# Convolving block 3 token-major in a pair with block 4, with the work around it reordered

## The chip, the cores and the metric

The kernel runs on one core of one Trainium2 chip. The metric is the device time of one execution in microseconds. A core has five engines that run side by side and wait for each other through semaphores: TensorE (PE, matrix products into PSUM), VectorE (DVE), ScalarE (ACT), GpSimd (POOL) and SyncE (SP, which here issues nearly all DMAs). "PEld" in a profile is the loading of weights into PE, which overlaps its products.

## The reference

Two steps follow each other. The first is a light causal convolution over time: x has 8 sequences of 4160 tokens with 192 channels, 8 heads of 24 channels each, and each head has 7 taps that a softmax turns into weights. The second is a feed-forward layer with a maximum of three branches.

```python
w = weight - np.max(weight, axis=-1, keepdims=True)
w = np.exp(w)
w = w / (np.sum(w, axis=-1, keepdims=True) + 1e-09)
x_pad = np.concatenate([np.zeros((B, pad, D)), x], axis=1)
idx = np.arange(S)[:, None] + np.arange(K)[None, :]
x_unf = x_pad[:, idx, :].reshape(B, S, K, H, group)
y = np.einsum('hk,bskhg->bshg', w, x_unf).reshape(B * S, D)
h = np.maximum(np.maximum(y @ w1, y @ w2), y @ w3)      # 192 -> 768
out = h @ w_out                                         # 768 -> 192
```

## The kernel before

The 33280 tokens are cut into 65 blocks of 512 (`NBLK`); block `t` is worked on in turn `t` of a loop that starts at 2, since blocks 0 and 1 are started by hand-written calls ahead of it. All work is in one program for five engines. The order on each engine is the order in which the Python code issues it: the kernel switches automatic scheduling off (`manual_schedule`).

**Convolution, two forms.** Blocks 0 to 3 (`NDENSE = 4`) are convolved densely: `cast_dense` casts x to 16 bit, `conv_dense` (L375) multiplies it with a band matrix in 80 products and gives y with channels on partitions, and `cross` copies half of it across partitions. From block 4 on the convolution is token-major: `cast_x` (L194, on POOL) casts the loaded tile `xf` to a tile `x16`, `conv` (L354) does 64 products for a whole `x16` tile (one block, a pair of blocks, or half the heads of four blocks), `evac` (L394) copies the PSUM tiles `G` to `ys`, `turn` (L408) has SP issue two DMA transposes from `ys` to `yp`, and `double` (L417, on POOL) makes the copy of `yp` in which the two halves of the partitions are swapped. Block 4 is alone in its tile, then pairs (5, 6), (7, 8) and so on follow, and blocks from 13 (`QUADS`) on go by fours. Token-major tiles need rows of zeros between the loaded ones; `zero_x` writes them once into each of the buffers `xf`.

**First product of the feed-forward layer** (`l1`, L500). The maximum of three branches is computed from differences of weights (`wd`). For each of 6 chunks (`j`) of 128 hidden units, three products of 64 rows go into a PSUM tile `lp` and three into `lq`; the two "lanes" use the upper and lower half of the PE rows, at the same time. `top` then evacuates: ACT makes `r = relu(lp)` (L487), DVE makes `h = max(r, lq)` (L488). `lp` lies in pool `psp` and `lq` in pool `psq`, each with 2 buffers of one bank.

**Second product** (`st2`, L564). A block takes 60 products of 192 columns, 30 in each lane, into tiles `po` of pool `psw` (4 buffers); `total` adds the lanes (ACT copy L571, DVE addition L572) for tokens 0 to 255 and for 256 to 511. `st2(t, (a, b))` issues what is left up to product a of lane 0 and b of lane 1.

**Interleaving.** In turn t the loop issues `l1(t, j)` for the six chunks and, after each, a share of `st2(t - 1)`: `EVEN = [5, 10, ..., 30]` or, in a turn with a late convolution, `ROOM`. The lists `convs_at`, `casts` and `loads` say in which turn a block is convolved, cast and loaded; `load_on` issues the loads. `meet()` empties both lanes before other PE work is issued. In turn 2 the kernel before calls `conv_dense(3)` after chunk 1 and `conv` of block 4 after chunk 3; in turn 3, after chunk 1, `conv` of the pair (5, 6).

**Start.** ACT exponentiates the taps and DVE normalises them into `line`; 38 small PE products (L280) spread `line` over `band`, which the convolutions use. `keep_warm` runs products on zeros while PE waits.

Of the kernel before, what the change touches and what calls it, by code (L numbers as in the profile page):

```python
# [10 lines left out]
FP32 = mybir.dt.float32  # L11
# [5 lines left out]
KW = 7  # L17
PAD = KW - 1
NHEAD = 8
# [9 lines left out]
def kernel(  # L29
# [53 lines left out]
                            o_lo - (row_lo - S)))  # L83
        return res

    NDENSE = 4
    chunks_of = [conv_chunks(blk) for blk in blocks[:NDENSE]]
    NQ = len(chunks_of[0])
    TOK = 32
# [28 lines left out]
    def get_x(t):  # L118

        if not 0 <= t < NB or t in xin:  # L120
            return
        if t < XBUF:
            xbuf.append(const.tile([P, NR, D], FP32, name=f"xf_{t}"))
        xf = xbuf[t % XBUF if t < NDENSE + XBUF else NDENSE + (t - NDENSE - XBUF) % 3]
        assert all(v[0] is not xf for v in xin.values())
        xin[t] = [xf, 0, ()]

    def zero_x(t, q0=0, q1=NR, eng=None):

        if t >= NDENSE:  # L130
            get_x(t)
        xf = xbuf[t]
        if eng is not None:
            eng.memset(xf[TOK:HALF, q0:q1, :], 0.0)
            return
        zero = idle[TOK:HALF, 0:D]
        nc.scalar.copy(out=xf[TOK:HALF, q0:q1, :],
                       in_=bass.AP(tensor=zero.tensor, offset=zero.offset,
                                   ap=[list(zero.ap[0]), [0, q1 - q0], [1, D]]))

    def load_x(t, eng=nc.sync):
        if not 0 <= t < NB:
            return
        loaded.add(t)
        get_x(t)
        xf = xin[t][0]
        if t < NDENSE:
            todo = [(0, c[3], c[1] * SEQ + c[2], i) for i, c in enumerate(chunks_of[t])]
        else:
            todo = [(HALF * (i // NR) + (0 if s else LAP), KR if s else TOK,  # L150
                     b * SEQ + s - (LAP if s else 0), i % NR) for i, (b, s) in enumerate(rows_of(t))]
        parts = []
        i, n = 0, len(todo)
        row = [c[2] for c in todo]
        while i < n:
            k = i
            while k + 1 < n and todo[k + 1][:2] == todo[i][:2] and row[k + 1] - row[k] == row[i + 1] - row[i]:
                k += 1
            step = row[i + 1] - row[i] if k > i else 0
            p0, rlen, _, q0 = todo[i]  # L160
            q1 = todo[k][3] + 1
            src = bass.AP(tensor=x.tensor, offset=row[i] * D,
                          ap=[[D, rlen], [step * D, q1 - q0], [1, D]])
            eng.dma_start(out=xf[p0:p0 + rlen, q0:q1, :], in_=src)  # L164
            if parts and parts[-1][0] == rlen:
                parts[-1] = (rlen, parts[-1][1], q1)
            else:
                parts.append((rlen, q0, q1))
            i = k + 1
        xin[t] = [xf, todo[0][0], parts]  # L170

    pairs = {NDENSE: (NDENSE, 0, 1)}
    for t in range(NDENSE + 1, NB):
        u = (t - NDENSE - 1) % 2 if t < QUADS else (t - QUADS) % 4
        pairs[t] = (t - u, u, 2 if t < QUADS else 4)

    def place(t):
# [19 lines left out]
    NC, NSLOT, CYC = D // HALF, D // 32, 96  # L197
    NCH = NC * NBLK // P
    xz = {t: [const.tile([P, NQ, D], FP16, name=f"xz_{t}_{v}") for v in range(2)] for t in range(2)}
    xz[2], xz[3] = xz[0], xz[1]  # L200

    def cast_dense(t, copies, slots_=range(CYC // 32)):
        xf, _, parts = xin.pop(t)
        for v, copy in enumerate(copies):
            if copy is None:
                continue
            for s in slots_:
                cut = GRP * (32 * s // GRP + 1)
                a, b = (32 * s, cut) if v == 0 else (cut, 32 * s + 32)
                for (rl, q0, q1) in parts:  # L210
                    copy(  # L211
                        out=xz[t][v][0:rl, q0:q1, :].rearrange("p q (k c) -> p q k c", c=CYC)[:, :, :, a:b],
                        in_=xf[0:rl, q0:q1, :].rearrange("p q (k c) -> p q k c", c=CYC)[:, :, :, a:b])
# [23 lines left out]
    load_wb(slice(PW, DFF))  # L237
    load_wa(slice(2 * PW, DFF))
    nc.sync.dma_start(out=wos[:], in_=moe_w_out.rearrange("(j p) c -> p j c", p=P))
    load_x(2)  # L240
    load_x(3)
    ident = const.tile([P, P], FP32)
    make_identity(nc, ident[:])
    ident16 = const.tile([P, P], FP16)
    nc.gpsimd.tensor_copy(out=ident16[:], in_=ident[:])
    idle = const.tile([P, NBLK], FP16)
    nc.vector.memset(idle[:], 0.0)
    def keep_warm(n, pool=psw, tag="w"):
# [13 lines left out]
    band = const.tile([P, NHEAD, BAND_W], FP16)  # L262
    nc.vector.memset(band[:], 0.0)
    keep_warm(5, psp, "p")
    wexp = const.tile([NHEAD, KW], FP32)
    wsum = const.tile([NHEAD, 1], FP32)
    nc.scalar.activation(out=wexp[:], in_=wk[:], func=AF.Exp, accum_out=wsum[:])
    wrec = const.tile([NHEAD, 1], FP32)
    nc.vector.reciprocal(out=wrec[:], in_=wsum[:])
    zero_x(4)  # L270
    nc.vector.tensor_scalar_mul(out=line[:, 31:31 + KW], in0=wexp[:], scalar1=wrec[:])
    for v in range(2):
        nc.vector.memset(xz[1][v][:], 0.0)
    cast_dense(0, (nc.vector.tensor_copy, nc.vector.tensor_copy))
# [133 lines left out]
                nc.sync.dma_start_transpose(out=yp[:, 0, i, :, :, :].rearrange("p u k n -> p (u k) n"),  # L408
                                            in_=slots[t][:, i, v:v + n, :, :].rearrange("p u r d -> p (u r d)"))

    def double(t):

        if not NDENSE <= t < NB:
            return
        yp = dense[t]
        for i in range(2):
            nc.gpsimd.tensor_copy(out=yp[HALF * i:HALF * (i + 1), 1, :, :, :, :].rearrange("p i u k n -> p (i u k n)"),  # L417
                                  in_=yp[HALF * (1 - i):HALF * (2 - i), 0, :, :, :, :].rearrange("p i u k n -> p (i u k n)"))

    def spot(t, i, c, r):  # L420

# [32 lines left out]
    def op(fn):  # L454
        ops.append((tuple(put), fn))
# [21 lines left out]
    def meet():  # L477

        emit(True)
        assert not ops  # L480
        clock[0] = clock[1] = 0
# [194 lines left out]
    zero_x(6, 4, NR, nc.vector)  # L676
    conv_dense(0, (ACT, DVE))
    zero_x(6, 0, 4)
    for t in range(NDENSE, XBUF):
        load_x(t)  # L680
    copy_w3(DVE, 0, 2)
    make_wd(2, 0, 2)
# [24 lines left out]
    l1_dense([(1, 4, WW), (1, 5, WW)], "HF")  # L707
    tops((1, 4), (1, 5))
    transpose_w3((PQ[0], PQ[0], PQ[1]))
    cast_dense(3, (GP, GP))  # L710
    cross_wd(1, ACT)
    first_hidden(0)
    first_hidden(1)
# [4 lines left out]
    make_m(1)  # L718
    zero_x(0, NQ)
    zero_x(2, NQ, NR, nc.vector)  # L720
    zero_x(3, NQ, NR, nc.vector)
    load_x(7)
    cast_x(5)

    convs_at = {2: 4, 3: 5, 4: 7}
    convs_at.update({t - 3: t for t in range(9, QUADS, 2)})
    convs_at.update({t - 4 + i: t for t in range(QUADS, NB, 4) for i in range(2)})
    casts = {4: 9}  # L730
# [5 lines left out]
    def load_on(t):  # L736
        for v in range(loads[t - 1] + 1, loads[t] + 1):
            if v not in loaded:
                load_x(v)

    EVEN = [5, 10, 15, 20, 25, 30]
    ROOM = [5, 13, 17, 21, 26, 30]
    OWN, AHEAD = 3, 4
    for t in range(2, NB):
        u = convs_at.get(t, NB)
        late = t > 2 and u < NB
        if t in (3, 4):
            double(t + 1)
        if t > 3:
            for v in range(casts.get(t - 1, 8) + 1, casts[t] + 1):  # L750
                cast_x(v)
        l1(t, 0)
        if t == 2:
            first_rest()
        elif t == 3:
            cast_x(8)
            nc.gpsimd.tensor_copy(out=m16[0:HALF, 2, :], in_=m16[HALF:P, 0, :])
            nc.gpsimd.tensor_copy(out=m16[HALF:P, 2, :], in_=m16[HALF:P, 1, :])
        if t > 3 and not late:
            op(lambda t=t: (store(t - 2, 0, 4, (nc.sync,)),  # L760
                            turn(t + 2, (2,)) if place(t + 2)[1:] == (0, 4) else None, load_on(t)))
        else:
            op(lambda t=t: store(t - 2, 0, 4, (nc.sync,)))
        cuts = ROOM if late else EVEN
        st2(t - 1, (cuts[0], cuts[0]))
        for j in range(1, NJ):
            l1(t, j)
            if late and j == 1:
                st2(t - 1, (cuts[0] + OWN + AHEAD, cuts[0] + OWN))
                meet()  # L770
                quad, second = u >= QUADS, u < QUADS or t == u - 3
                conv(u, WPWQ, range(4 * second, 4 * second + 4) if quad else range(NHEAD))
                for i in (0, 2):
                    evac(u, i)
                for i in (1, 3):
                    evac(u, i, nc.vector.tensor_copy)
                if second:
                    turn(u)
                load_on(t)
            if t == 2 and j == 1:  # L780
                meet()
                conv_dense(3, (ACT, DVE))
                zero_x(1, NQ, NR, nc.vector)
                cross(3, GP)
                load_x(8)
                cast_x(6)
            elif t == 2 and j == 3:
                meet()
                conv(u, WW)
                evac(u, 0)  # L790
                evac(u, 1, nc.vector.tensor_copy)
                turn(4)
                load_x(9)
                cast_x(7)
            st2(t - 1, (cuts[j], cuts[j]))
            if j == 1 and t > 4 and t + 2 in pairs and pairs[t + 2][1] % 2 == 0:
                double(t + 2)
            if t == NB - 1 and j == 3:
                op(lambda: store(NB - 2, 0, 2, (nc.sync,)))
        if t == NB - 1:  # L800
            op(lambda: store(NB - 2, 2, 4, (nc.sync,)))
    last(NB - 1)
# [28 lines left out]
```

## Time and profile before

| | |
|---|---|
| device time, median of 3 runs | 454.51 us (454.46 to 455.02) |
| span of the profiled execution (no own time is given beside it) | 452.8 us |
| median less that span | 1.7 us |
| PE busy | 446.9 us, 99% |
| DVE, ACT, POOL busy | 356.7, 320.0 and 203.0 us |
| granted TensorE clock, mean | 0.999 |

The profile is of one execution. A row of the timeline gives start and length in us, engine, line of the code, operation, output and input, partitions and shape, count, and in brackets how long the engine was idle before it and what ended that. Lengths of PE products include a tail in which the next product already runs, so the cost on PE is read from start to start.

### The profile page before, as it was taken

Reading aid. Unit: us, or ns where it says so; the run is one execution under the profiler, and the core shown is the slowest. Engines: PE = TensorE matmul, PEld = TensorE weight load, DVE = VectorE, ACT = ScalarE, POOL = GpSimd, SP = SyncE. Lnnn points to the kernel's source line nnn. Section 1 sums busy time; section 2 is a strip of 40 time slices with the busy share of each in tenths; the row PEclk is TensorE's granted clock in tenths of the full one; section 3 lists DMA queues with packets and bytes.
Section 4 is the critical chain, followed back from the end, with each engine's and each line's share of the span. In section 5 each row is a group of like instructions: output and inputs, shape, how many; then the busy total and the mean of one; then the engine's idle time right before and its main releaser. Section 6 shows DMA issues by size and latency. Waiting matters only on the chain.

```text
span 452.8 us, 18491 instructions
## 1 busy us (share of the span) xinstructions
PE 446.9 (99%) x7702; PEld 411.5 (91%) x7702; DVE 356.7 (79%) x614; ACT 320.0 (71%) x605; POOL 203.0 (45%) x226
## 2 busy tenths in 40 slices
PE   8999999999999999999999999999999999999997
PEld 4569999999999999999999999999999999999996
DVE  7767778878878788887878788887878788787775
ACT  7767767767777676777767677776767777776664
POOL 2774836556454444635353363444346452504000
PEclk9999999999999999999999999999999999999999
DMA  7978977597966958497585958958594876435223
GB/s 205 231 186 152 225 188 196 143 202 184 171 177 141 178 127 225 123 175 183 119 189 143 192 137 161 199 137 182 135 213 115 178 189 119 116 88 104 59 72 106
DMA packets 127987, 72.03 MB, mean 159 GB/s; under 512 B 52064, under 2 KB 127711, under 8 KB 127903
## 3 DMA queue, kind: packets, MB, share of 16 engines
q1 hardware_dynamic: 127743, 70.75, 69.4%
q8 instruction: 60, 0.98, 1.0%
q14 instruction: 24, 0.20, 0.2%
q10 hardware_dynamic: 160, 0.10, 0.1%
HBM read 33.28 MB, written 25.56 MB: 130 GB/s over the span
## 4 chain that ended last, share of the span: by engine, by line
PE 96%; SPq 2%; DMA 1%; issue 0%; POOL 0%; DVE 0%; POOLq 0%
PE po L564 36%; PE lq L500 31%; PE lp L500 22%; PE G L354 3%; DMA ws<-in_moe_w_dram 1%; PE lw L523 1%; SPq L227 1%; SPq L223 1%; PE D L375 1%; PE po L622 0%; PE po L595 0%; PE lp L523 0%; SPq L164 0%; PE pm L334 0%; POOL wd L299 0%
## 5 line engine op out<-in xcount | busy, mean ns | idle before, releaser
L564 PE MATMUL po<-wo,h 64*128 64x192 f16 x3024 | 331.3, 243 | 0.7 <-issue 0.7
L488 DVE TENSOR_TENSOR h<-r,lq 128x512 f16<-128x512 f16 x384 | 263.0, 686 | 85.9 <-ACT r L487 78.2
L487 ACT ACTIVATE r<-lp 128x512 f16<-128x512 f32 x384 | 229.0, 597 | 115.1 <-PE lp L500 101.8
L500 PE MATMUL lp<-yp,wd 64*128 64x512 f16 x1098 | 295.7, 376 | 0.0
L500 PE MATMUL lq<-yp,wd 64*128 64x512 f16 x1098 | 295.5, 376 | 0.0
L564 PEld LDWEIGHTS <-h 64*128 64x128 f16 x3024 | 241.6, 94 | 6.8 <-issue 4.9
L500 PEld LDWEIGHTS <-wd 64*128 64x128 f16 x2268 | 179.1, 94 | 12.3 <-issue 0.2
L194 POOL CAST x<-xf 103x768 f16<-103x768 f32 x122 | 97.5, 827 | 107.5 <-DMA xf<-in_x_dram 82.0
L564 PE MATMUL po<-m,yp 64*128 64x192 f16 x720 | 141.1, 243 | 0.0
L417 POOL COPY yp<-yp 64x1536 f16<-64x1536 f16 (+1 forms) x62 | 89.6, 1445 | 95.9 <-DMA yp<-ys 70.6
L572 DVE TENSOR_TENSOR o<-a,po 128x384 f32<-128x384 f32 x126 | 69.0, 547 | 0.0
L564 PEld LDWEIGHTS <-yp 64*128 64x128 f16 x720 | 66.3, 94 | 0.3
L571 ACT COPY a<-po 128x384 f32<-128x384 f32 x126 | 59.5, 473 | 0.0
L394 ACT CAST ys<-G 128x384 f16<-128x384 f32 x61 | 26.3, 482 | 9.6 <-PE G L354 9.6
L394 DVE CAST ys<-G 128x384 f16<-128x384 f32 x61 | 31.0, 550 | 0.0
L354 PE MATMUL G<-x,band 39*32 39x192 f16 (+2 forms) x1152 | 17.3, 234 | 0.0
L354 PEld LDWEIGHTS <-band 39*32 39x32 f16 x1152 | 10.7, 91 | 5.2 <-issue 4.7
L500 PE MATMUL lp<-yd,wd 64*128 64x512 f16 x36 | 9.7, 376 | 0.0
L500 PE MATMUL lq<-yd,wd 64*128 64x512 f16 x36 | 9.7, 376 | 0.0
L211 POOL CAST xz<-xf 112x160 f16<-112x160 f32 (+2 forms) x15 | 4.4, 339 | 8.8 <-DVE w3s L303 7.6
L523 PEld LDWEIGHTS <-wd 128*128 128x128 f16 (+1 forms) x48 | 3.0, 96 | 5.6 <-issue 2.2
L375 PEld LDWEIGHTS <-xz 112*32 112x32 f16 x320 | 4.7, 107 | 3.3 <-POOL xz L211 1.3
(72 smaller groups left out, 97.6 us busy)
## 6 DMA issues: line engine op xcount, KB each, us to landing
xf<-in_x_dram SPq DMA_DIRECT2D x113, 234.0 KB
out_dram<-o SPq DMA_DIRECT2D x62, 384.0 KB
xf<-in_x_dram SPq DMA_DIRECT2D x7, 204.8 KB
xf<-in_x_dram SPq DMA_DIRECT2D x3, 420.0 KB
ws<-in_moe_w_dram SPq DMA_DIRECT2D x8, 128.0 KB
yp<-ys SPq DMA_TRANSPOSE x62
out_dram<-o SPq DMA_DIRECT2D x5, 192.0 KB
wos<-in_moe_w_out_dram SPq DMA_DIRECT2D x1, 576.0 KB
```

What stands on the lines that cost most here:

```text
L194: nc.gpsimd.tensor_copy(out=x16s[t0][0:K, :, :, u, r, :].rearrange("p h j c -> p j h c"), in_=xf[0:K, 4 * r:4 * r + 4, :].rearrange("p j ( ...
L354: nc.tensor.matmul(G[2 * (k // per) + i][TOK * j:TOK * (j + 1), k % per, :], lhsT=band[row, h, HALF * i + LAP:HALF * i + KR], rhs=x16s[t0] ...
L375: nc.tensor.matmul(ps[32 * g:32 * g + 32, lo:hi], lhsT=xz[t][v][0:rlen, q, 32 * s:32 * s + 32], rhs=band[0:rlen, h, cc:cc + hi - lo], star ...
L394: copy(out=slots[t][:, i % 2, :, :, GRP * h0:GRP * (h0 + per)].rearrange("p u r (h c) -> p h (u r) c", c=GRP), in_=G[i][:].rearrange("p h ...
L417: nc.gpsimd.tensor_copy(out=yp[HALF * i:HALF * (i + 1), 1, :, :, :, :].rearrange("p i u k n -> p (i u k n)"), in_=yp[HALF * (1 - i):HALF * ...
L487: nc.scalar.activation(out=r[:], in_=ps[0][:], func=AF.Relu)
L488: nc.vector.tensor_max(out=hs[t][:, j, :], in0=r[:], in1=ps[1][:])
L500: nc.tensor.matmul(ps[i][:], lhsT=w_of(i, c, j), rhs=y_all(t, i, c), start=(n == 0), stop=(n == NC - 1))
L523: nc.tensor.matmul(open_ps[t, j, i][:], lhsT=a, rhs=b, start=(t, j, i) not in begun, stop=(t, j, i) in begun)
L564: nc.tensor.matmul(ps[b0, i][:, s % 2, :], lhsT=a, rhs=b, start=first, stop=last)
L571: nc.scalar.copy(out=a[:], in_=ps[s - 1, 0][:])
L572: nc.vector.tensor_add(out=outs[t][:, s - 1:s + 1, :], in0=a[:], in1=ps[s - 1, 1][:])
```

## The change

- `NDENSE` becomes 3. Block 3 is loaded in the token-major layout (its zeros written by POOL near the start, `zero_x(3, eng=nc.gpsimd)`), cast by `cast_x`, and shares one tile with block 4: one `conv(3, ...)` in turn 2 after chunk 1 gives both, into four tiles `G`, evacuated by ACT and DVE, two each. The convolution of block 4 alone and the dense one of block 3 with its `cross` are gone.
- At the end of turn 2 new calls follow: the convolution of the pair (5, 6), its transposes, then the doubling copies of pair (3, 4), the first on POOL and the second on DVE, with the whole second stage of block 2 issued in two halves around the second copy. In turn 3 there is then no `st2(2)` left, so its six chunks of `l1` are issued with nothing between.
- SP's queue: the transposes of block 3 stand ahead of the load of x for block 8, those of the pair 5 ahead of the store of block 1.
- The softmax subtracts the maximum (a DVE reduction ahead of the exponential) and adds 1e-9 to the sum (an eighth column that holds 1e-9, summed by a DVE reduction in place of the accumulator of ACT).

```diff
-    NDENSE = 4
+    NDENSE = 3
...
-    pairs = {NDENSE: (NDENSE, 0, 1)}
-    for t in range(NDENSE + 1, NB):
-        u = (t - NDENSE - 1) % 2 if t < QUADS else (t - QUADS) % 4
+    pairs = {}
+    for t in range(NDENSE, NB):
+        u = (t - NDENSE) % 2 if t < QUADS else (t - QUADS) % 4
...
-    load_x(2)
-    load_x(3)
     ident = const.tile([P, P], FP32)
...
+    load_x(2)
+    zero_x(3, eng=nc.gpsimd)
+    load_x(3)
...
-    nc.scalar.activation(out=wexp[:], in_=wk[:], func=AF.Exp, accum_out=wsum[:])
+    wexp = const.tile([NHEAD, KW + 1], FP32)
+    nc.vector.memset(wexp[:], 1e-9)
+    wneg = const.tile([NHEAD, 1], FP32)
+    nc.vector.reduce_max(out=wneg[:], in_=wk[:], axis=AXX, negate=True)
+    nc.scalar.activation(out=wexp[:, 0:KW], in_=wk[:], func=AF.Exp, bias=wneg[:])
     wrec = const.tile([NHEAD, 1], FP32)
-    nc.vector.reciprocal(out=wrec[:], in_=wsum[:])
+    nc.vector.reduce_sum(out=wrec[:], in_=wexp[:], axis=AXX)
+    nc.vector.reciprocal(out=wrec[:], in_=wrec[:])
...
-    def double(t):
+    def double(t, copies=(nc.gpsimd.tensor_copy,) * 2):
...
-    cast_dense(3, (GP, GP))
+    cast_x(3)
...
-    zero_x(3, NQ, NR, nc.vector)
...
-    convs_at = {2: 4, 3: 5, 4: 7}
+    convs_at = {4: 7}
...
-        late = t > 2 and u < NB
-        if t in (3, 4):
-            double(t + 1)
+        late = u < NB
+        if t == 4:
+            double(5)
...
-            op(lambda t=t: store(t - 2, 0, 4, (nc.sync,)))
+            op(lambda t=t: (store(t - 2, 0, 4, (nc.sync,)), load_on(t) if t == 3 else None))
...
             if t == 2 and j == 1:
                 meet()
-                conv_dense(3, (ACT, DVE))
+                conv(3, WPWQ)
+                for i in range(2):
+                    evac(3, i, ACT)
+                    evac(3, i + 2, DVE)
+                turn(3)
                 zero_x(1, NQ, NR, nc.vector)
-                cross(3, GP)
                 load_x(8)
                 cast_x(6)
             elif t == 2 and j == 3:
-                meet()
-                conv(u, WW)
-                evac(u, 0)
-                evac(u, 1, nc.vector.tensor_copy)
-                turn(4)
                 load_x(9)
                 cast_x(7)
...
+        if t == 2:
+            meet()
+            conv_all(5)
+            turn(5)
+            double(3, (GP, None))
+            st2(2, (15, 15))
+            double(3, (None, DVE))
+            st2(2, (30, 30))
+            meet()
```

`conv_all(t)` is the pair's convolution into `psw`, `psp`, `psw` and `psq`, evacuated by ACT (first and third tile) and DVE (second and fourth), as the loop did before.

More of the change, by code (lines that the diff above doesn't have):

```diff
@@ L123, in get_x @@
             xbuf.append(const.tile([P, NR, D], FP32, name=f"xf_{t}"))
-        xf = xbuf[t % XBUF if t < NDENSE + XBUF else NDENSE + (t - NDENSE - XBUF) % 3]
+        xf = xbuf[t % XBUF if t < XBUF + 4 else 4 + (t - XBUF - 4) % 3]
         assert all(v[0] is not xf for v in xin.values())
@@ L199 @@
     xz = {t: [const.tile([P, NQ, D], FP16, name=f"xz_{t}_{v}") for v in range(2)] for t in range(2)}
-    xz[2], xz[3] = xz[0], xz[1]
+    xz[2] = xz[0]
     def cast_dense(t, copies, slots_=range(CYC // 32)):
@@ L264 @@
     keep_warm(5, psp, "p")
-    wexp = const.tile([NHEAD, KW], FP32)
-    wsum = const.tile([NHEAD, 1], FP32)
-    nc.scalar.activation(out=wexp[:], in_=wk[:], func=AF.Exp, accum_out=wsum[:])
+    wexp = const.tile([NHEAD, KW + 1], FP32)
[3 more added lines that the diff above has]
+    nc.scalar.activation(out=wexp[:, 0:KW], in_=wk[:], func=AF.Exp, bias=wneg[:])
     wrec = const.tile([NHEAD, 1], FP32)
-    nc.vector.reciprocal(out=wrec[:], in_=wsum[:])
+    nc.vector.reduce_sum(out=wrec[:], in_=wexp[:], axis=AXX)
+    nc.vector.reciprocal(out=wrec[:], in_=wrec[:])
     zero_x(4)
-    nc.vector.tensor_scalar_mul(out=line[:, 31:31 + KW], in0=wexp[:], scalar1=wrec[:])
+    nc.vector.tensor_scalar_mul(out=line[:, 31:31 + KW], in0=wexp[:, 0:KW], scalar1=wrec[:])
     for v in range(2):
@@ L415, in double @@
         yp = dense[t]
-        for i in range(2):
-            nc.gpsimd.tensor_copy(out=yp[HALF * i:HALF * (i + 1), 1, :, :, :, :].rearrange("p i u k n -> p (i u k n)"),
-                                  in_=yp[HALF * (1 - i):HALF * (2 - i), 0, :, :, :, :].rearrange("p i u k n -> p (i u k n)"))
+        for i, copy in enumerate(copies):
+            if copy is None:
+                continue
+            copy(out=yp[HALF * i:HALF * (i + 1), 1, :, :, :, :].rearrange("p i u k n -> p (i u k n)"),
+                 in_=yp[HALF * (1 - i):HALF * (2 - i), 0, :, :, :, :].rearrange("p i u k n -> p (i u k n)"))
     def spot(t, i, c, r):
@@ L678 @@
     zero_x(6, 0, 4)
-    for t in range(NDENSE, XBUF):
+    for t in range(NDENSE + 1, XBUF):
         load_x(t)
@@ L739, in load_on, with conv_all @@
                 load_x(v)
+    def conv_all(t, heads=range(NHEAD)):
+        conv(t, WPWQ, heads)
+        for i in (0, 2):
+            evac(t, i)
+        for i in (1, 3):
+            evac(t, i, DVE)
     EVEN = [5, 10, 15, 20, 25, 30]
@@ L771 @@
                 quad, second = u >= QUADS, u < QUADS or t == u - 3
[L772 to L776, printed above, removed]
+                conv_all(u, range(4 * second, 4 * second + 4) if quad else range(NHEAD))
                 if second:
```

## The prediction

> **What bounds the kernel now.** I read the page first, then the stretches by engine, then the timelines of PE, ACT, DVE, POOL and SP from 20 to 50 us, where all moved work lies, and last the built order of the changed kernel, which lists each engine's instructions with the engines they wait for. The page:
>
> ```profile
> PE 446.9 (99%) x7702; PEld 411.5 (91%) x7702; DVE 356.7 (79%) x614; ACT 320.0 (71%) x605; POOL 203.0 (45%) x226
> PE 96%; SPq 2%; DMA 1%; issue 0%; POOL 0%; DVE 0%; POOLq 0%
> ```
>
> The second line is the chain that ended last: 96% PE. The stretches by engine (PE, PEld, DVE, ACT, POOL busy, clock, DMA):
>
> ```profile
> 24.00:42.00 18.00, 17.18 (x414) 13.28 (x413) 13.03 (x23) 11.58 (x24) 11.84 (x18) 1.00 0.75 163
> 58.00:445.00 387.00, 387.00 (x6522) 366.30 (x6509) 310.31 (x523) 276.26 (x523) 167.42 (x168) 1.00 0.69 154
> ```
>
> From 58 to 445 us PE is never idle, so what PE gains or loses before that is carried to the end one for one; nothing later gives it back. The change acts between 24 and 42 us. PE there, from its timeline (start, length):
>
> ```profile
> 26.68 1.43 PE L375 MATMUL D<-band,xz 112*32 112x103 f16 x80
> 28.03 0.42 PE L564 MATMUL po<-wo,h 64*128 64x192 f16 x5
> ...
> 30.26 0.67 PE L354 MATMUL G<-x,band 39*32 39x48 f16 x64
> 30.86 0.54 PE L564 MATMUL po<-m,yd 64*128 64x192 f16 x3
> ...
> 33.13 0.26 PE L564 MATMUL po<-wo,h 64*128 64x192 f16 x2 [0.68 <-issue]
> ...
> 34.46 0.38 PE L500 MATMUL lp<-yd,wd 64*128 64x512 f16 x1
> ...
> 36.83 0.75 PE L354 MATMUL G<-x,band 39*32 39x96 f16 x64
> 37.52 0.25 PE L564 MATMUL po<-wo,h 64*128 64x192 f16 x1
> ```
>
> Starts matter, since matmuls overlap: dense convolution of block 3, 28.03 - 26.68 = 1.35 us; narrow token-major one of block 4, 30.86 - 30.26 = 0.60; wide one of a pair, 37.52 - 36.83 = 0.69. An l1 chunk (six products, two lanes) takes 3 x 0.215 = 0.65 us from start to start, ten st2 products 29.52 - 29.11 = 0.41. So PE repeats 1.06 us per chunk. The evacuation of a chunk, from the timelines of ACT and DVE:
>
> ```profile
> 38.45 0.60 ACT L487 ACTIVATE r<-lp 128x512 f16<-128x512 f32 x1 [0.26 <-PE lp L500]
> ...
> 39.08 0.69 DVE L488 TENSOR_TENSOR h<-r,lq 128x512 f16<-128x512 f16 x1 [0.47 <-ACT r L487]
> ```
>
> Relu frees lp, 0.63 us later the maximum starts and frees lq at its end. psp and psq have two buffers each.
>
> **Saved on PE.** Dense 1.35 + narrow 0.60 are replaced by one wide convolution, 0.69 (blocks 3 and 4 are a pair now): 1.26 saved. The pair 5 and 6 moves from block 3's turn to the end of block 2's, still 0.69. Two waits fall away: 0.68 at 33.13, which no wait or row explains, and 0.27 between 30.86 and 31.14, where second-stage products waited after the narrow convolution. The first could return elsewhere: 0 to 0.68, and I take 0, because PE's next long wait (below) covers the same moment. Saved: 1.26 + 0.68 + 0.27 = 2.2.
>
> **New waits in block 2.** Conv of 3 starts at 26.68 as before: its second input, x of block 4, was cast by 24.21 + 1.60 = 25.81, and x of block 3 takes 1.60 in place of 1.71 on POOL. The convolution ends at 27.37, ten st2 products at 27.78. Chunk (2,2)'s second lane then needs the lq of chunk (2,1), freed at 27.41 + 0.69 = 28.10: 0.3 lost. DVE now evacuates two tiles and zeroes xf there as well, so I add 0.1 for small waits up to chunk 5. Four chunks at 1.06 from 28.1 and those 0.1 give 32.5 for the end of l1 and of block 1's second stage (before: 34.46).
>
> **New wait ahead of st2 of block 2.** The pair's convolution fills 32.5 to 33.2. Then 60 st2 products run with no l1 between. Their second lane takes the bank that block 1's last addition frees. DVE order: the maximum of (2,5), then that addition. The last product of (2,5) ends near 32.2, relu starts 32.23, maximum 32.86, addition 0.60 later at 33.46, 0.55 long: 34.0. PE waits 0.85. The 60 products, 2 x 30 x 0.041 = 2.46, run to 36.5.
>
> **New wait ahead of block 3.** Block 3 was dense and needed no transpose; now l1 needs both transposes and both doubling copies. SP issues the transposes once DVE has evacuated, from about 28.65 (its queue holds only the store before them; the next x load moves behind). From issue to the waiting copy took 37.44 - 31.51 = 5.9 and 44.71 - 38.22 = 6.5, so y lands at 34.6 to 35.2. POOL's copy (half of the 2.99 for two) ends by 36.7, on PE's heels. DVE's copy is the later one: it is queued behind the addition of block 2's first half. That half ends on PE at 34.0 + 1.23 + 0.24 = 35.5, ACT's copy takes 0.47, the addition 0.55, so 36.5. The DVE copy of 64x1536 has no row. Bounds: 0.42 (a 64x512 copy, 0.83 for two) and 3 x 0.42 = 1.25. DVE casts of 80 and 240 elements last 0.19 and 0.285, so a fixed part of about 0.15 is in each; 0.15 + 3 x 0.27 = 0.95, which I take. l1 of block 3 starts at 37.45, PE having been free at 36.5: 0.95 lost. Maxima of block 3 queue behind this copy, but they come later anyway.
>
> The Trainium skill, "VectorE: DVE Perf Modes", section "The perf-mode tier table", gives 693 ns for a 2048-element 16-bit SBUF copy. By it 1536 elements would take an estimated 0.6 us and the sum would fall by about 0.4; the rows for 512 elements are slower than that rate, so I stay with them.
>
> **New waits inside block 3.** The built order shows its six chunks in a row and no st2 between: second stage of 2 is used up, that of 3 cannot start. Each chunk's first two products carry waits there:
>
> ```
> lp0_3_2 <- yp_3, wd [waits Activation]
> lq1_3_2 <- yp_3, wd [waits DVE]
> ```
>
> Chunk n+2 needs the lq that chunk n's maximum frees. From a chunk's first q product: lp's last product starts 0.22 later, lasts 0.38, relu starts 0.03 after it, maximum 0.63 after that, 0.69 long, 0.03 to the next product: 1.98 per two chunks, where PE has 1.29 of work. Before, ten st2 products filled this gap. Three such rounds fall due, at chunks (3,2), (3,4) and (4,0): 3 x 0.69 = 2.05. After (4,0) st2 of block 3 fills the gaps again.
>
> **At no cost.** The softmax chain gets a memset, two reductions and a longer path, but loses an accumulator read: with small DVE rows at 0.12 to 0.22, weights come about 0.5 later. PE's convolution of block 0 moves from 6.27 to 6.8; its four products then end near 9.6, where PE waits for POOL's cast of block 1 until 9.65 anyway. If that cover fails, 0.1 to 0.3. POOL's memset of xf 3 lies in its 7.6 us of idle time before 9.27. Pair 5's transposes are issued earlier and used 7 us after block 3 starts; x loads 8 and 9 come later on SP, 10 earlier, and conv of 7 needs 8 only in block 4.
>
> **Sum.** Waits 0.4 + 0.85 + 0.95 + 2.05 = 4.25, minus 2.2 saved: +2.05. The execution profiled has a span of 452.8, so 454.8; the 1.7 between that span and the median 454.51 stays: 456.5. About 0.2% (0.9 us) is what a measurement of this kernel can tell from no change.
>
> **Rivals.** First: no slower, because the rounds in block 3 do not bind. If banks were freed earlier than the instructions end (DVE rows 0.69 long start 0.60 apart, relus about 0.50), a round could shrink; at 1.29 all 2.05 go and the time is 454.5. It decides once a round is under about 1.6. Starts 0.63 apart between relu and its maximum in every steady chunk speak against it: the steps depend on each other. With every wait at its least (0.5, 0.5, 1.5, 0.1) it is 454.5 + 0.4 = 454.9. Chance 0.16, of which 0.05 for clearly faster.
>
> Second: worse, because y of 3 arrives late. DMA queues are 75% busy here and x of 7, the store and the transposes share them. POOL's copy binds instead of DVE's when y lands after 36.0. Landing 1.5 us later than 36.0 adds 1.5: 458.0. The two rows of 5.9 and 6.5 speak against it, with 0.8 to spare. The unexplained 0.68, should it return, gives 457.2, and the copy at 1.25 another 0.3. Chance 0.16.
>
> The Trainium skill, "TensorE: Matmul & The Clock Gate", section "A second HAM failure mode: psum-queue depth-cycling", speaks against the change: small idle gaps between matmul groups can make the clock drop. This trace shows 1.00 granted from 24 to 42 us with the 0.68 gap in it, and products of 0.38 on both sides of it. By the rule, half rate over block 3's 3.9 us of work would add up to 3.9, an estimate; no part of the sum uses it.
>
> **How the numbers follow.** Forecast 456.5, chance 0.68. The range reaches from the least waits, 454.9, rounded to 455.0, to the late landing, 458.0, plus rounding: 458.2. Faster 0.05, same 0.11, slower 0.84.
>
> **What would show it.** In the changed profile: dense products x240, G all 96 wide; l1 of block 2 ending near 32.5; PE idle about 0.85 before po of block 2, waiting for DVE; l1 of block 3 starting near 37.5, released by DVE's 64x1536 copy and not by POOL's; three PE gaps of 0.7 in block 3, released by the maximum; clock 1.00. I am wrong if block 3's chunks follow each other at 0.65, or if PE waits at block 3 for POOL or a DMA.

## The result, and the profile after

The changed kernel took 457.31 us (median of 4 runs, 455.91 to 457.61), the kernel before 454.49 beside it (4 runs, 453.12 to 455.02): a ratio of 1.0056, 95% interval 1.0037 to 1.0075, slower by some 2.5 us. The forecast was 456.5, with a range of 455.0 to 458.2. The execution profiled has a span of 455.8 us and a time of 457.61.

Busy time and the chain, from the page of the changed kernel:

```profile
PE 447.8 (98%) x7622; PEld 409.8 (90%) x7622; DVE 357.9 (79%) x617; ACT 320.0 (70%) x604; POOL 202.9 (45%) x220
PE 95%; DVE 2%; ACT 1%; issue 1%; DMA 0%; DVEq 0%; ACTq 0%
```

PE has 80 products fewer, and DVE and ACT now hold 3% of the chain, where before DVE had 0% and ACT was not in it. The stretches by engine say where. First the part that the change rearranges, from the first l1 product of block 2 to the first product of conv of 7, before and then after; the last line is the steady part, after:

```profile
24.16:43.98 19.82, 19.00 (x441) 15.03 (x441) 14.62 (x26) 13.00 (x25) 11.81 (x17) 1.00 0.76 162
```

```profile
25.90:47.10 21.20, 19.30 (x361) 12.24 (x361) 15.05 (x26) 12.99 (x25) 11.08 (x14) 1.00 0.92 172
58.00:445.00 387.00, 387.00 (x6560) 367.28 (x6557) 310.40 (x524) 276.34 (x523) 168.29 (x168) 1.00 0.70 154
```

PE is again never idle from 58 to 445 us, and from conv of 7 to the end it took 408.7 us, against 408.8 before. So all of it happens ahead of conv of 7, as forecast: 1.38 us in this section, and 1.74 us ahead of it (block 2 starts at 25.90 instead of 24.16). The section holds idle time now: 21.20 less 19.30 busy. PE's timeline shows where (start, length, idle time before it and who ended it):

```profile
28.42 0.83 PE L358 MATMUL G<-x,band 39*32 39x96 f16 x64
...
29.60 0.38 PE L506 MATMUL lp<-yd,wd 64*128 64x512 f16 x1
29.89 0.37 PE L506 MATMUL lq<-yd,wd 64*128 64x512 f16 x1
...
31.85 0.32 PE L570 MATMUL po<-wo,h 64*128 64x192 f16 x2
32.26 0.37 PE L506 MATMUL lq<-yd,wd 64*128 64x512 f16 x1
...
34.47 0.75 PE L358 MATMUL G<-x,band 39*32 39x96 f16 x64
35.15 0.25 PE L570 MATMUL po<-m,yd 64*128 64x192 f16 x1
35.80 0.26 PE L570 MATMUL po<-m,yd 64*128 64x192 f16 x2 [0.40 <-DVE o L578]
...
38.21 0.38 PE L506 MATMUL lp<-yp,wd 64*128 64x512 f16 x1
38.87 0.37 PE L506 MATMUL lq<-yp,wd 64*128 64x512 f16 x1 [0.29 <-DVE yp L423]
...
40.17 0.37 PE L506 MATMUL lp<-yp,wd 64*128 64x512 f16 x1
40.89 0.37 PE L506 MATMUL lq<-yp,wd 64*128 64x512 f16 x1 [0.35 <-DVE h L494]
...
42.91 0.37 PE L506 MATMUL lq<-yp,wd 64*128 64x512 f16 x1 [0.35 <-DVE h L494]
...
44.92 0.37 PE L506 MATMUL lq<-yp,wd 64*128 64x512 f16 x1 [0.35 <-DVE h L494]
```

Read the starts, not the idle time in brackets: a product is busy for 0.37 but hands over to the next after 0.02 to 0.2, so a bracket of 0.35 is a loss of about 0.7 (40.89 - 40.17 = 0.72, where 0.02 is usual). Five waits stand there, each released by the engine that the prediction named: block 1's last addition ahead of st2 of block 2 (35.15 to 35.80), DVE's copy ahead of block 3 (38.21 to 38.87), and three times the maximum in block 3, 2.02 us apart. Inside block 2 two smaller waits have no bracket and show in the starts alone: 29.60 to 29.89 and 31.85 to 32.26. DVE's rows there, and at the copy:

```profile
29.15 0.69 DVE L494 TENSOR_TENSOR h<-r,lq 128x512 f16<-128x512 f16 x1 [0.32 <-ACT r L493]
...
30.95 0.54 DVE L134 MEMSET xf<- 32x576 f32 x1 [0.17 <-issue]
31.52 0.69 DVE L494 TENSOR_TENSOR h<-r,lq 128x512 f16<-128x512 f16 x1
...
37.68 0.56 DVE L578 TENSOR_TENSOR o<-a,po 128x384 f32<-128x384 f32 x1 [1.00 <-ACT a L577]
38.27 0.56 DVE L423 COPY yp<-yp 64x1536 f16<-64x1536 f16 x1
```

Both waits of block 2 end within 0.05 us of the end of a maximum (29.84 and 32.21), the second of which stood behind the zeroing of xf. The copy is queued behind the addition, as forecast, and lasts 0.56 us.

### The profile page after: what moved, and what is told of

Its sections match the earlier page's. It is cut to its first block, busy times and chain, and to the rows that moved or that the text cites. A ratio compares the mean times of both kernels' runs of the same rounds, so it can differ in the third digit from the quotient of the medians.

```text
span 455.8 us, 18325 instructions
## 1 busy us (share of the span) xinstructions
PE 447.8 (98%) x7622; PEld 409.8 (90%) x7622; DVE 357.9 (79%) x617; ACT 320.0 (70%) x604; POOL 202.9 (45%) x220
## 4 chain that ended last, share of the span: by engine, by line
PE 95%; DVE 2%; ACT 1%; issue 1%; DMA 0%; DVEq 0%; ACTq 0%
PE po L570 35%; PE lq L506 32%; PE lp L506 21%; PE G L358 3%; PE lw L529 1%; DVE h L494 1%; PE lp L529 1%; PE D L379 1%; PE po L628 0%; PE po L601 0%; PE lq L529 0%; DMA wk<-in_weight_dram 0%; ACT xf L137 0%; ACT band L288 0%; ACT L270 0%
## 5 line engine op out<-in xcount | busy, mean ns | idle before, releaser
L570 PE MATMUL po<-wo,h 64*128 64x192 f16 x3024 | 327.6, 243 | 0.0
L506 PE MATMUL lq<-yp,wd 64*128 64x512 f16 x1116 | 299.9, 376 | 1.3 <-DVE h L494 1.1
L506 PE MATMUL lp<-yp,wd 64*128 64x512 f16 x1116 | 300.6, 376 | 0.0
L506 PEld LDWEIGHTS <-wd 64*128 64x128 f16 x2268 | 177.0, 94 | 15.8 <-issue 4.1
L570 PE MATMUL po<-m,yp 64*128 64x192 f16 x732 | 143.2, 243 | 0.0
L423 POOL COPY yp<-yp 64x1536 f16<-64x1536 f16 x61 | 89.4, 1466 | 96.8 <-DMA yp<-ys 49.3
L358 PE MATMUL G<-x,band 39*32 39x192 f16 (+1 forms) x1152 | 17.4, 235 | 0.1
L506 PE MATMUL lp<-yd,wd 64*128 64x512 f16 x18 | 5.1, 378 | 0.0
L529 PE MATMUL lw<-yd,wd 64*128 64x512 f16 (+1 forms) x24 | 5.1, 379 | 0.0
```

The costliest lines, as they stand in the source:

```text
L358: nc.tensor.matmul(G[2 * (k // per) + i][TOK * j:TOK * (j + 1), k % per, :], lhsT=band[row, h, HALF * i + LAP:HALF * i + KR], rhs=x16s[t0] ...
L506: nc.tensor.matmul(ps[i][:], lhsT=w_of(i, c, j), rhs=y_all(t, i, c), start=(n == 0), stop=(n == NC - 1))
L529: nc.tensor.matmul(open_ps[t, j, i][:], lhsT=a, rhs=b, start=(t, j, i) not in begun, stop=(t, j, i) in begun)
L570: nc.tensor.matmul(ps[b0, i][:, s % 2, :], lhsT=a, rhs=b, start=first, stop=last)
```

## The experiments

Open after the first result: whether the 1.74 us ahead of block 2 come from the softmax; whether block 3's rounds really cost what their gaps show; and what the 0.68 us wait was that stood in the profile before and is missing in the profile after. Theory: block 3's rounds, which run at the latency of a bank's evacuation, make nearly the whole loss. Rivals: the softmax's longer chain makes it (A), or the rounds only lack work to fill them.

**The softmax alone.** Kernel before, with the new softmax:

```
-wexp = const.tile([NHEAD, KW], FP32)
-wsum = const.tile([NHEAD, 1], FP32)
-nc.scalar.activation(out=wexp[:], in_=wk[:], func=AF.Exp, accum_out=wsum[:])
+wexp = const.tile([NHEAD, KW + 1], FP32)
+nc.vector.memset(wexp[:], 1e-9)
+nc.vector.reduce_max(out=wneg[:], in_=wk[:], axis=AXX, negate=True)
+nc.scalar.activation(out=wexp[:, 0:KW], in_=wk[:], func=AF.Exp, bias=wneg[:])
...
+nc.vector.reduce_sum(out=wrec[:], in_=wexp[:], axis=AXX)
```

> The kernel before with the new softmax alone; blocks, order and loads as before. Theory A (the 1.7 us that the changed kernel is late at the first l1 product of block 2, 25.90 against 24.16, come from the softmax: the table load stands behind the wait for the taps, 2.47 against 1.38, the weights come 1.3 later, PE idles 1.2 at 3.5 us and its products of 512 columns start 0.43 apart instead of 0.22 until about 10.5): 1.4 to 1.9 us slower than before, PE's first small product near 4.7, l1 of block 2 near 25.8. Theory B (the start is late through x of block 3 in two loads, POOL's memset and slower landings, 10.31 against 9.14 for x of block 1): at most 0.4 slower, l1 of block 2 by 24.6.

454.84 against 454.68, ratio 1.0006 (0.9993 to 1.0018). A is out: 0.3 us by the ratio, at most 0.8 by its interval.

**Everything but the softmax.** Changed kernel, with the lines above the other way round.

> The changed kernel with the old softmax (no maximum, sum by ACT's accumulator); the rest as changed. Theory A: 1.4 to 1.9 faster than the changed kernel, so about 1.2 slower than before, all of it between 24 and 42 us; l1 of block 2 starts by 24.3. Theory B: at most 0.4 faster than the changed kernel and l1 of block 2 still starts after 25.

456.92 against 454.68, ratio 1.0055 (1.0035 to 1.0074). The loss stays without the softmax.

**The table loaded early.** The traces show why the weights come late at all. ACT's rows, before and after:

```profile
1.38 1.28 ACT L267 ACT_TABLE_LOAD   x1 [1.38 <-PEq L815]
```

```profile
2.47 1.28 ACT L270 ACT_TABLE_LOAD   x1 [2.47 <-DMA wk<-in_weight_dram]
```

The exponential now takes two inputs from elsewhere, and its table load stands behind the wait for the taps, where before it ran while they were on their way. In the changed kernel a one-element exponential was put ahead of it:

```
+early = const.tile([1, 1], FP32)
+nc.scalar.activation(out=early[:], in_=idle[0:1, 0:1], func=AF.Exp)
```

> The changed kernel with one exponential of a single zero put on ACT ahead of the softmax, so that the table is loaded before the wait for the taps. Theory A with the table load as its main part: the load starts near 1.4, the exponential of the taps near 2.9 instead of 3.76, PE's idle time at 3.5 us falls from 1.2 to 0.3 or 0.4, the products speed up as early as before, and 1.0 to 1.7 us are won. If the two reductions are what costs: 0.3 or less. Theory B: nothing.

457.99 (456.10 to 461.61) against 454.68, ratio 1.0084 (1.0052 to 1.0116). The load is back at 1.38 and the band products start at 3.88 instead of 4.74, yet nothing is won: PE then stands for 1.17 us, from start to start, ahead of block 1's convolution at 10.48.

**Four pairs of banks in block 3.** Its odd chunks use the pool `psw`:

```
-            l1(t, j)
+            l1(t, j, WW if t == 3 and j % 2 else PQ)
```

> The changed kernel with chunks 1, 3 and 5 of block 3's l1 in the four buffers of psw, which are free there, in place of psp and psq; so a chunk waits for the maximum four or more chunks back. Theory C (each round of two chunks waits 0.7 for the maximum because two buffers are too few): the three gaps of 0.7 go, chunks follow at 0.65, 1.8 to 2.1 us faster than the changed kernel. Rival D (DVE at 0.60 to 0.69 per maximum is the next limit, or psw is released late): the chunks follow at 0.8 or more, at most 1.0 faster.

454.42 against 454.68, ratio 1.0001 (0.9988 to 1.0014): the loss is gone, 2.5 us by the two ratios. In its PE timeline chunks of block 3 follow each other at 0.65 and no wait is left inside the block (`lw` is psw's):

```profile
38.21 1.00 PE L506 MATMUL lw<-yp,wd 64*128 64x512 f16 x6
38.86 0.38 PE L506 MATMUL lp<-yp,wd 64*128 64x512 f16 x1
...
39.50 1.00 PE L506 MATMUL lw<-yp,wd 64*128 64x512 f16 x6
40.15 0.38 PE L506 MATMUL lp<-yp,wd 64*128 64x512 f16 x1
```

This won more than forecast, 2.5 where the three gaps make 2.1; the difference is within the intervals.

**The changed kernel again,** as it is:

> The changed kernel itself, once more, beside the three below on one chip. If the late first l1 product of block 2 in its first profile (25.90) belongs to the kernel, it is again past 25.4 and the time 2.8 over before. If it belongs to that one execution, as 24.19 with the same start in the kernel with four buffer pairs suggests, the product starts at 24.0 to 24.9, and the span is 2.0 to 2.7 over before, most of it between that product and block 7's convolution (21.2 us against 19.8 before).

456.62 against 454.44, ratio 1.0051 (1.0029 to 1.0072). This profile starts block 2 at 24.39, not 25.90, and its section lasts 21.19 again. So most of the 1.74 us ahead of block 2 belongs to one execution.

**The rounds filled.** In the changed kernel the second half of block 2's second stage is spread over block 3's chunks instead of standing ahead of them:

```
-        cuts = ROOM if late else EVEN
+        cuts = [18, 20, 23, 25, 28, 30] if t == 3 else ROOM if late else EVEN
...
-            st2(2, (30, 30))
```

> The changed kernel, but the second half of block 2's second stage (30 products, 1.23 us) issued between the chunks of block 3, some 5 after each, instead of ahead of it. If the rounds are bound by the time that two evacuations take (2.02 us for two chunks), the products fit into the gaps, chunks follow at the same starts and block 3 starts when DVE's copy lets it, as before: same time as the changed kernel or up to 0.4 faster. If PE's own work binds there: 1.2 slower.

456.66 against 454.44, ratio 1.0050 (1.0030 to 1.0070): no gain. Its PE timeline:

```profile
36.55 0.37 PE L506 MATMUL lp<-yp,wd 64*128 64x512 f16 x1 [0.73 <-POOL yp L423]
37.49 0.37 PE L506 MATMUL lq<-yp,wd 64*128 64x512 f16 x1 [0.57 <-DVE yp L423]
...
39.03 0.33 PE L570 MATMUL po<-wo,h 64*128 64x192 f16 x2
39.51 0.37 PE L506 MATMUL lq<-yp,wd 64*128 64x512 f16 x1
...
41.52 0.37 PE L506 MATMUL lq<-yp,wd 64*128 64x512 f16 x1
```

Inside block 3 the products fill the rounds, and a round still takes 2.02 us (37.49, 39.51, 41.52): its length is the latency of product, relu and maximum, whatever PE does in it. What was put in there is missing ahead of block 3, where PE now waits for both copies. Five products per chunk make 2 x (0.65 + 5 x 0.041) = 1.7 us of work per round, still under 2.02; ten, as the kernel before has, make 2.1. The waits are moved, not removed.

**Four pairs, and DVE's copy earlier:**

```
-            l1(t, j)
+            l1(t, j, WW if t == 3 and j % 2 else PQ)
...
-            double(3, (GP, None))
+            double(3, (GP, DVE))
             st2(2, (15, 15))
-            double(3, (None, DVE))
```

> Four buffer pairs in block 3, and DVE's swapped copy of y of 3 and 4 issued ahead of the second stage of block 2 instead of in its middle, so that it no longer stands behind the addition of the first half. Theory: block 3's l1 waits 0.29 to 0.45 for that copy; with it early, POOL's copy (about 1.5 after y lands) is the last, ready when PE is free: the wait goes, 0.3 to 0.5 faster than with four pairs alone. Rival: y lands later than DVE's evacuation of the pair 5 and 6, DVE stands still for it and the additions behind it come late: same or 0.3 slower.

453.95 against 454.44, ratio 0.9990 (0.9974 to 1.0006). The wait ahead of block 3 is gone. DVE's copy now runs beside POOL's; DVE's row, then POOL's:

```profile
35.60 1.14 DVE L423 COPY yp<-yp 64x1536 f16<-64x1536 f16 x1
```

```profile
34.87 1.46 POOL L423 COPY yp<-yp 64x1536 f16<-64x1536 f16 x1 [2.34 <-DMA yp<-ys]
```

The same copy that took 0.56 takes 1.14, twice as long, and DVE has time for it there.

**And later cuts in block 2,** so that block 1's second stage ends a chunk earlier and its last addition is not waited for:

```
+        cuts = [5, 10, 16, 23, 30, 30] if t == 2 else ROOM if late else EVEN
```

> As the kernel before this one, and the second stage of block 1 issued faster in block 2's turn (10, 16, 23, 30, 30 of 30 after chunks 1 to 5), so that its last addition stands ahead of the last maximum on DVE. Theory: the wait of 0.6 to 0.75 on that addition at the start of block 2's second stage goes: 0.5 to 0.7 faster than without it, about 453.5. Rival: the second stage of block 2 then waits for the last maximum instead (h of chunk 5 is needed six products in): 0.2 or less.

454.11 against 454.44, ratio 0.9986 (0.9967 to 1.0004). The wait for the addition (33.94 to 34.69 in the two kernels with four pairs before it) is gone, but the 0.5 to 0.7 us did not come in the time: 453.95 had been reached without the cuts. In this profile PE lost 0.7 us elsewhere, between its starts at 25.16 and 25.88, waiting for the second of two copies on DVE beside which POOL was casting, and 0.9 more at 75.56, a wait without a name (below):

```profile
25.88 0.37 PE L506 MATMUL lq<-yd,wd 64*128 64x512 f16 x1 [0.35 <-DVE yd L390]
```

**The same once more, and with the old softmax.** Both were run beside the kernel before.

> The version with four pairs, the early copy and the later cuts once more, beside the one with the old softmax. Theory: 453.9 to 454.4, ratio 0.998 to 1.000, within 0.1 of its first result; then 20 fast runs and more decide whether it beats the kernel before by more than 0.2%. Rival (its first result of 0.9986 was the spread of single runs): 1.000 to 1.001.

> The last version (four pairs in block 3, the early copy, the later cuts), now also with the old softmax. If the reading of the second half holds, the three waits are gone for good and what is left of the change is the token-major convolution without its waits: its section from the first l1 of block 2 to conv of 7 took 18.5 us against 19.8 before, of which 0.9 to 1.1 may be a wait that comes and goes. Theory (the waits were the whole loss, the softmax is worth nothing within 0.4): 453.7 to 454.3, ratio 0.998 to 1.000. Rival (the new softmax costs its 0.3 to 0.4 after all, hidden so far in the spread): 453.2 to 453.6, ratio 0.997 to 0.998, and faster than before by more than its interval.

454.11 against 454.56, ratio 0.9980 (0.9955 to 1.0005), and 454.71, ratio 0.9999 (0.9981 to 1.0017). Neither beats the kernel before by more than its interval, and the old softmax wins nothing: its time lies above both theories' ranges, its ratio at the upper end of the first. The section of the latter is the shortest of all, 17.78 us with PE busy for 17.68:

```profile
24.61:42.39 17.78, 17.68 (x363) 13.48 (x362) 15.34 (x26) 13.05 (x25) 11.03 (x16) 1.00 0.95 181
```

**The wait without a name.** The 0.68 us at 33.13 in the profile before, which no semaphore explains, is found again in most profiles, at other places. PE's rows in the runs with the softmax alone, four pairs, later cuts again, and the old softmax with them:

```profile
28.64 0.34 PE L378 MATMUL D<-band,xz 112*32 112x103 f16 x13 [0.39 <-issue]
```

```profile
28.57 0.26 PE L570 MATMUL po<-wo,h 64*128 64x192 f16 x2 [0.76 <-issue]
```

```profile
29.34 0.26 PE L570 MATMUL po<-wo,h 64*128 64x192 f16 x2 [1.33 <-issue]
```

```profile
75.03 0.25 PE L567 MATMUL po<-wo,h 64*128 64x192 f16 x1 [0.91 <-issue]
```

Counted over all PE records, products and weight loads, in order of time, the first three stand at number 961, the fourth at 2753, and the one before at 1217: 961 + 256 = 1217, 1217 + 6 x 256 = 2753. All other such waits stand at 961 or 2753 too. The page has a queue for instructions (of the changed kernel: packets, MB, share of 16 engines):

```profile
q8 instruction: 59, 0.97, 0.9%
```

0.97 MB in 59 packets is 16 KB each. The kernel before has 60 such packets. Its page counts 7702 products and as many weight loads, 60.2 times 256; the changed kernel's 7622 make 59.5. The Trainium skill, "Runtime: NRT & Kernel Launch", section "Instruction fetch mechanics", says that instructions come in blocks of 16 KiB, 256 instructions, and that crossing a boundary is mostly hidden. Packets and places agree. If the fetch is the cause, most crossings are hidden here too, since only three of some sixty places ever show a wait; but those waits are 0.6 to 1.6 us long from start to start. Ten of the twelve profiles have one or two, the two of the changed kernel itself none. No run here moved a boundary on purpose, so that the fetch is the cause is read from the places and packets, not tested.

## Why the prediction was right

The sign and the mechanism held, and the priced waits came where they were written; that the total came so near was in part luck, as the sum below shows. Its timetable against the profile after, from the first l1 product of block 2 on:

| stretch | forecast | measured |
|---|---|---|
| to conv of 5 | 32.5 - 24.16 = 8.34 | 34.47 - 25.90 = 8.57 |
| conv of 5 and the wait for block 1's addition | 34.0 - 32.5 = 1.5 | 35.80 - 34.47 = 1.33 |
| 60 products of block 2 | 2.5 | 38.21 - 35.80 = 2.41 |
| held ahead of block 3 | 0.95 | 38.87 - 38.21 = 0.66 |
| three rounds | 3 x 1.98 = 5.94 | 44.92 - 38.87 = 6.05 |

**The rounds (2.05).** Measured 3 x (2.02 - 1.29) = 2.2. Four pairs take them away and the loss with them; filling them changes nothing. So they bind, by latency, and the first rival falls.

**Block 2 (0.4).** The two waits cost 0.29 and some 0.25: the first was priced at 0.3, the second, behind DVE's zeroing, stood in the sum with 0.1.

**DVE's copy (0.95).** The queueing was right: the addition ahead of it ends at 38.24, which is 12.34 us after the block's start, and the forecast had 36.5 - 24.16 = 12.34. The copy itself was mis-sized: 0.56, not 0.95. The prediction had the right price beside it, an estimate of 0.6 from the rate in the Trainium skill, "VectorE: DVE Perf Modes", section "The perf-mode tier table", and stayed with rows of 64x512 copies at 0.42. The kept profiles show why those rows are slow: POOL was casting beside them (22.31 to 24.02, the copies 23.33 to 24.16). In the profile with four pairs POOL stood still from 23.32 to 23.91, and the same two copies took 0.60 in place of 0.83:

```profile
23.38 0.60 DVE L390 COPY yd<-yd 64x512 f16<-64x512 f16 x2 [2.37 <-ACT yd L384]
```

With 0.29 for one copy, of which 0.15 is the prediction's own fixed part, 1536 elements come to 0.15 + 3 x 0.14 = 0.57. So the row was real and the wrong one to scale.

**The addition (0.85).** 35.15 to 35.80, 0.65 from start to start, some 0.6 lost. The addition came on time (9.85 after the block's start, forecast 9.84); PE came to it 0.2 later.

**Saved on PE (2.2).** The wide convolution took 29.18 - 28.42 = 0.76 for 0.69, and the second 0.68; saved 1.19 for 1.26. The 0.68 is the term that failed: it was booked as saved by the change, and a wait like it stands in ten of twelve profiles, of versions of both orders. Before's start gap of 32.21 to 33.13 cost 0.88 and flatters the section's difference: 21.20 - (19.82 - 0.88) = 2.26 without it, where the profiles side by side show 1.38. The kernel with the softmax alone gives the same base, 19.46 less its 0.58 = 18.88. The changed kernel's two profiles, 21.20 and 21.19, hold no such wait. With the old softmax and with the early table, where one falls into block 2, the section less that wait is 20.8 and 21.0; there it seems to cover part of block 2's own waits, so the change costs this section 1.9 to 2.3.

**The sum.** Without the credit the ledger has 4.25 - 1.53 = 2.7 for this section, where 2.26 was measured: 0.3 too much for the copy and 0.25 for the addition, 0.15 too little for the rounds and for block 2 each, 0.07 too little for the convolution, and some 0.3 of the difference not singled out. Two errors of opposite sign, a credit of 0.7 that was none and the rest 0.45 too dear, left 2.05 close to it: that is luck.

**The start (0).** The weights came 1.0 to 1.3 us later, not 0.5, for the table load behind the taps' DMA, which the prediction did not see. The cover mostly held: 0.3 us in the softmax's own run, with an interval of -0.3 to 0.8. 2.26 + 0.3 is 2.6; the two comparisons of the changed kernel gave 2.8 and 2.2, that with the old softmax 2.2.

**The second rival** (y of 3 late) does not decide in the changed kernel: PE is released there by DVE's copy. POOL's copy, at 36.08 and 1.47 long, ended 0.7 us before PE came. With less work ahead, in the filled version, POOL's copy binds at once (0.73). That margin was as thin as the prediction said.

**The clock.** 1.00 in the section, products of 0.37 to 0.39 on both sides of every gap: three gaps of 0.72 us, 2 us apart, did not bring the slower clock that the Trainium skill, "TensorE: Matmul & The Clock Gate", section "A second HAM failure mode: psum-queue depth-cycling", would allow for short idle gaps.

**Open.** The last version's section is 1.2 us shorter than before's 18.94 without its wait, yet its time is the same as before's within 0.2%. Its profiled execution gives the difference back in a wait of 1.2 us at 75.03 and a later start of block 2 (24.61). Whether that is so in the mean, the spread of its runs (452.84 to 456.97) hides.

## What to carry to other kernels

Before moving a block's filler work ahead of it, work out the block's round without filler: the latency from a bank's product to its release, divided by the number of banks. If PE's work is shorter than that, keep enough filler inside the round or give it more banks. Here the banks, one edit in one call, gave back all that the new order had lost; filling the rounds won nothing, since PE then came to the copies ahead of the block before they were done. Before scaling a row, see what ran beside it: the copy was priced from one that POOL slowed. And do not book a wait that no semaphore explains as saved: look for it in another execution first.

## What the runs showed of the hardware

- Waits of 0.6 to 1.6 us on PE that no semaphore explains, at PE record 961, 1217 or 2753, multiples of 256 apart. They come and go from profile to profile, all in the first 80 us.
- A 64x1536 copy on DVE takes 0.55 to 0.56 us alone. Where POOL's copy of the same shape still ran for its first 0.35, 0.48 or 0.73 us, it took 0.76, 0.89 and 1.14: each time longer by about the overlap less 0.14, so next to nothing gets done meanwhile.
- An activation that must wait for a DMA and another engine had its table load behind the wait: 2.47 instead of 1.38.
- At the start, products of 512 columns run 0.43 us apart, later 0.22. Before, 0.22 is reached at 8.46 (8.46, 8.67, 8.89); after, where PE had stood idle for 1.2 us ahead of 4.74, they are still 0.43 apart at 9.61, 10.04 and 10.47. The granted clock of both stretches reads 1.00, so that column doesn't show every slow product.
